# Attention and a routed MoE on one core: conditional weight loads, GpSimd drains, the left-over pass third, and the first slot's table and loads moved forward

## The chip, the core and the metric

The kernel runs on one core of one Trainium2 chip. The metric is device time in microseconds, the median of several runs. Engines are TensorE (PE, with its weight loads as PEld), VectorE (DVE), ScalarE (ACT), GpSimd (POOL) and SyncE (SP), which here only reads registers and issues DMAs. GpSimd issues the indirect DMAs (gathers and scatters by a list of row numbers).

## The reference

Sigmoid attention over 8 batches of 12 heads (448 positions, head size 64) gives x; each of its 3584 rows goes to the one expert of eight with the largest logit, through two matrices, and is scaled by two gates.

```python
# q, k, v: [8, 12, 448, 64]
scores = matmul(q, k.T) / sqrt(64) - log(448)
x = (sigmoid(scores) @ v).transpose(0, 2, 1, 3).reshape(3584, 768)
logits = x @ w_gate                       # [3584, 8]
e_idx = argmax(logits, axis=1)
gate_w = softmax(logits)[arange, e_idx]   # denominator + 1e-9
eom = sigmoid(x @ w_output_gate)
for e in range(8):
    mask = e_idx == e
    h = maximum(x[mask] @ w1[e], 0)       # 768 -> 1024
    out[mask] = gate_w[mask] * eom[mask, e] * (h @ w2[e])   # 1024 -> 768
```

## The kernel before

**Attention.** The work is 24 groups of two head pairs, each group seven units, 168 units in all, in one loop whose order is written out by hand. In turn `u` PE runs the scores of unit u (L540), ACT their sigmoid (L541), and PE the values of unit u-2 (L548). `evict` adds up and transposes a head pair's result (L561, L562); at a batch's end four DMAs write the batch to `x_dram` (L567). `gates(g-1)` runs in a group's fourth unit: PE multiplies the finished x by the gate weights `wg` (L580), and DVE adds that to `gl` (L584, L586). `load_qk` and `load_v` fetch two groups ahead.

**Routing.** `route(b)` is a generator whose steps the loop takes at fixed units: "logits" (L217 to L224), "counts" (L227 to L238), "places" (L240 to L252), "rows" (L254 to L260). The last one has GpSimd scatter the rows' numbers and gate values of batch b to the expert's region of a list in DRAM (`lst`, L258), four indirect DMAs. `init_list` fills that list beforehand.

**Slots.** The MoE part works in slots of 448 rows of one expert ("full") and of 256 rows ("part"). Two early full slots take rows of the first six batches only, so that slot 0 can be got ready while attention runs; the others are late ones. `table()` computes on DVE which expert and which place in the list each slot has. For a slot, `load_list` reads the place into an SP register and loads its list (L344), `spread_lists` copies it into `lts` and `lxs` on GpSimd (L351 to L354), `slot_regs` reads the expert into a register, `gather` fetches the rows (L363: 14 indirect DMAs for a full slot, 8 for a part slot), `turn_x` transposes them on DVE (L397). `load_w` loads weights into the raw area (L368), w1 and w2 in turn, since they share it. Every product is made as three: `split` makes a rounded part on ACT (L381) and the rest of it on DVE (L382).

**One slot.** `slot(cur, nxt)` starts with the gather of the next slot, then runs layer 1 in eight blocks f0 to f7 of 18 matmuls (L412 to L414, evicted by ACT L422 and DVE L423), meanwhile splitting the slot's own w2 and loading the next w1, then layer 2 in row tiles of 128 by two halves of 384 columns (L437 to L439, evicted by ACT L440), each tile scattered to `out` by GpSimd (L445), meanwhile turning and splitting the next x and w1 and loading the next w2. A full slot has 64 rows left over; `layer2_rest` (L458 to L461) takes them last.

**Slot 0.** Its steps stand inside the attention loop. In `unit(u)` u counts backward from the end of attention, -1 being the last unit with scores. The table's steps and the gather come from `before` and `after`, at the turn in which a pair index reaches `READY`: in the same count the table stands at -29 and -25, list 0 and the registers at -24, the gather at -22, list 1 at -18. w1 is loaded in six rows from -20 to -15 and split by rows at -15, -13, -11, -10, -3, -1; x is turned at -7, -6, -5 and split one unit later each. The loop ends with f0's matmuls of slot 0 (`layer1_mm`) and the last `gates`. The last batch's routing, the late table and the late lists come from the generator `side()`, one step between blocks of the first slots; its first step ("logits" of the last batch) is taken ahead of slot 0's `slot()` call, so between f0 and f1.

**Late and part slots.** How many there are is known at run time. At least two late slots always run; those beyond, and all part slots, are nested `tc.If` blocks (L716, L723), and behind each nest there is a join at which every engine brings its semaphores to the value that they would have with every block run. Each slot prefetches the one behind it, whether that exists or not. With these inputs two early, five late and two part slots run.

The functions that the diff touches:

Of the kernel before, what the change touches and what calls it, by code (L numbers as in the profile page):

```python
# [22 lines left out]
E = 8  # L23
# [21 lines left out]
READY = (EARLY_BATCH + 1) * NPAIR + 3  # L45
# [11 lines left out]
class Kernel:  # L57
# [67 lines left out]
    def constants(self):  # L125
# [11 lines left out]
        self.wg = cp.tile([128, NPAIR, D], F32, name="wg")  # L137
        nc.gpsimd.memset(self.wg, 0.0)
        nc.gpsimd.dma_start(self.wg[:, :, 0:16], self.wgo)
# [123 lines left out]
    def table(self, late):  # L263
# [8 lines left out]
        pos, tab = t([1, n, E]), t([1, 2, n])  # L272
# [24 lines left out]
        if late:  # L297
            ohb, tb, tmb = t([1, E, E]), t([1, 3, E]), t([1, E, E])
            bb = lambda a: a.unsqueeze(1).broadcast_to([1, E, E])
            slb = self.slots[:, 0, 0:E].unsqueeze(2).broadcast_to([1, E, E])  # L300
            tt(ohb, slb, bb(base[:, 1]), ALU.is_ge)
            tt(tmb, slb, bb(end[:, 1]), ALU.is_ge)
            tt(ohb, ohb, tmb, ALU.subtract)
            tt(tmb, ohb, bb(self.ids), ALU.mult)
            v.tensor_reduce(tb[:, 0], tmb, AX.X, ALU.add)
            tt(tmb, ohb, bb(sel[:, 1]), ALU.mult)
            v.tensor_reduce(tb[:, 1], tmb, AX.X, ALU.add)
            yield 1
# [9 lines left out]
        v.tensor_reduce(tab[:, 1], pos, AX.X, ALU.add)  # L318
        if late:
            first = t([1, n])  # L320
            v.tensor_scalar(first, self.slots[:, 0, 0:n], end[:, 0, E - 1:E], 0.0, ALU.is_equal, ALU.add)
            for i in range(2):
                v.scalar_tensor_tensor(tab[:, i], first, tb[:, i, 0:1], tab[:, i], ALU.mult, ALU.add)
            yield 1
        tabi = keep("tabi", [1, 2, n], I32)
        v.tensor_copy(tabi, tab)
        if late:
            tot, tbi = keep("tot", [1, 2], I32), keep("tbi", [1, 2, E], I32)
            v.tensor_copy(tot, end[:, :, E - 1])
            v.tensor_copy(tbi, tb[:, 0:2])  # L330
            self.tab_l, self.tab_b, self.tot = tabi, tbi, tot
        else:
            self.tab_e = tabi
# [33 lines left out]
    def load_w(self, s, src, dst, c, n):  # L367
        self.nc.sync.dma_start(  # L368
            dst[:, c:c + n],
            src[bass.ds(s["e"], 1), 128 * c:128 * c + 128 * n].rearrange("a (c p) f -> p (a c) f", p=128))  # L370
# [78 lines left out]
    def layer2_rest(self, s):  # L449
        nc = self.nc  # L450
        lt, (ya, yb) = s["lt"], self.ys
        lo, hi = slice(0, 64), slice(64, 128)
        for n in range(2):
            c = slice(384 * n, 384 * n + 384)
            ps = self.take("y", self.psy)[:, 0:384]
            for f in range(8):
                h = self.hr[:, f]
                nc.tensor.matmul(ps, h, self.w2h[:, f, c], start=(f == 0), stop=False)  # L458
                nc.tensor.matmul(ps, h, self.w2l[:, f, c], start=False, stop=(f == 7))
            nc.scalar.activation(yb[lo, c], ps[hi], AF.Copy, scale=r32(lt[hi, 3, 1:2]))  # L460
            nc.vector.scalar_tensor_tensor(ya[lo, c], ps[lo], r32(lt[lo, 3, 1:2]), yb[lo, c], ALU.mult, ALU.add)  # L461
        self.scatter(lt[lo, 3, 0:1], ya[lo])

    def slot(self, cur, nxt, side=None, begun=False):
        nx = None
        if begun:
            for k in range(4):
                self.load_w2(cur, k)
        if nxt is not None:
            nx = self.slot_regs(*nxt[:4])  # L470
            self.gather(nx, *nxt[4:])
        n = 32 * cur["lx"].shape[1]
# [14 lines left out]
        for i in range(2 * (n // 128)):  # L487
            t = i // 2
            self.layer2(cur, t, i % 2, self.ys[t % 2])
            if i == 0:  # L490
                self.split_x(nx, 2)
            if i < 3 and nx is not None:
                self.split_w1(i)
                for k in range(i, 4 if i == 2 else i + 1):
                    self.load_w2(nx, k)
            if side is not None and i > 0:
                next(side, None)
        if n % 128:
            self.layer2_rest(cur)
        return nx  # L500

    def attention(self, pool):
# [13 lines left out]
        self.es = self.scratch = t("es", [128, 1024])  # L516
        half = [slice(0, 64), slice(64, 128)]
# [59 lines left out]
        def gates(g):  # L577
            gp = self.ps_o[1]
            for h, e in corners:
                nc.tensor.matmul(gp[h][half[e], 0:S], self.wg[half[h], (G * g + e) % NPAIR], xts[e][half[h]],  # L580
                                 start=True, stop=True)
# [19 lines left out]
        for u in range(U * NG + LAG):  # L601
# [3 lines left out]
            if i == 0 or i == 4:  # L605
                self.before(G * g + i // 4)
# [14 lines left out]
            if i == 3 or i == 6:  # L621
                self.after(G * g + i // 4)
# [4 lines left out]
    def before(self, n):  # L627
        if n == READY + 2:
            self.early_slot()

    def unit(self, u):
        s = self.s0 if u > -21 else None
# [6 lines left out]
        for k in range(3):  # L639
            if u == -6 + k:  # L640
                self.split_x(s, k)
            if u == -7 + k:
                self.turn_x(s, k)
# [6 lines left out]

    def early_slot(self):
        self.early_lists(0, 1)
        self.s0 = self.slot_regs(self.tab_e, 0, self.lts[:, 0], self.lxs[:, 0])

    def after(self, n):
        if n == 2:
            self.init_list()
        if n == READY:
            self.tgen = self.table(False)
        if n == READY or n == READY + 1:  # L660
            for _ in range(2 - (n - READY)):
                next(self.tgen)
        if n == READY + 2:
            self.gather(self.s0, ROWS_E)
        if n == READY + 3:
            self.early_lists(1, EARLY)

    def build(self, phases="abc"):
# [14 lines left out]
        early = lambda k: (self.tab_e, k, self.lts[:, k], self.lxs[:, k], ROWS_E)  # L683
        late = lambda k: (self.tab_l, k, self.lts[:, EARLY + k], self.lxs[:, EARLY + k])

        def side():
            for _ in rt:
                yield
            yield
# [15 lines left out]
        next(sd)  # L705
# [15 lines left out]
        mid = lambda k: (self.tab_b, k, self.ltb[:, k], self.lxb[:, k])  # L721
# [41 lines left out]
```

## Time and profile before

| | us |
|---|---|
| median of 3 runs | 822.64 (822.46 to 823.29) |
| profiled run | 823.52 |
| its span | 821.7 |
| PE busy | 786.4 (96% of the span) |
| DVE, ACT, POOL busy | 380.7, 376.1, 287.1 |
| PE's first matmul of slot 0 (L412) starts | 298.56 |
| PE's first matmul of the first part slot starts | 732.00 |
| last scatter is issued | 802.58 |

Everything below is read from the one profiled execution. PE is the engine that is nearly always busy. The granted clock of PE over the span is 0.979 of full speed; it is lower where the page's row PEclk shows less than 9. A row of waits names the engine that waited, its line, and the engine and line whose work ended the wait.

### The profile page before, as it was taken

Reading aid. Unit: us, or ns where it says so; the run is one execution under the profiler, and the core shown is the slowest. Engines: PE = TensorE matmul, PEld = TensorE weight load, DVE = VectorE, ACT = ScalarE, POOL = GpSimd, SP = SyncE. Lnnn points to the kernel's source line nnn. Section 1 sums busy time; section 2 is a strip of 40 time slices with the busy share of each in tenths; the row PEclk is TensorE's granted clock in tenths of the full one; section 3 lists DMA queues with packets and bytes.
Section 4 is the critical chain, followed back from the end, with each engine's and each line's share of the span. In section 5 each row is a group of like instructions: output and inputs, shape, how many; then the busy total and the mean of one; then the engine's idle time right before and its main releaser. Section 6 shows DMA issues by size and latency. Waiting matters only on the chain. (4 is left out here: it accounts for less than half of the span.)

```text
span 821.7 us, 14599 instructions
## 1 busy us (share of the span) xinstructions
PE 786.4 (96%) x5748; PEld 598.7 (73%) x5748; DVE 380.7 (46%) x578; ACT 376.1 (46%) x437; POOL 287.1 (35%) x499
## 2 busy tenths in 40 slices
PE   9999999999999779999999999999999999989990
PEld 4444444444344349999999999999999999979990
DVE  1454444444454663925525615605615614616650
ACT  5656656666655632624424514514523523515540
POOL 5021213122135773128728027036136035124520
PEclk9999999999999988999999999999999999999995
DMA  8465664746667445562655346346345335425653
GB/s 289 123 169 137 186 147 141 202 114 162 159 175 214 145 101 189 164 206 60 196 199 180 123 150 202 107 139 207 100 141 202 119 126 197 141 95 183 236 204 131
DMA packets 75365, 132.78 MB, mean 162 GB/s; under 512 B 15487, under 2 KB 53375, under 8 KB 75280
## 3 DMA queue, kind: packets, MB, share of 16 engines
q1 hardware_dynamic: 64672, 106.47, 42.7%
q0 software_dynamic: 9680, 24.53, 9.3%
q8 instruction: 49, 0.80, 0.4%
q10 hardware_dynamic: 928, 0.69, 0.4%
q14 instruction: 36, 0.29, 0.1%
HBM read 108.77 MB, written 23.09 MB: 160 GB/s over the span
## 5 line engine op out<-in xcount | busy, mean ns | idle before, releaser
L541 ACT ACTIVATE a<-ps,bias_s 128x896 f32<-128x896 f32 x168 | 168.9, 1007 | 106.3 <-PE ps L540 106.3
L548 PE MATMUL ps<-a,v 64*64 64x448 f32 x1344 | 160.0, 542 | 3.9 <-ACT pc L240 3.9
L540 PE MATMUL ps<-q,k 64*64 64x448 f32 x1344 | 159.6, 544 | 2.4 <-ACT a L541 2.4
L412 PE MATMUL ps<-rounded 128*128 128x448 f32 (+1 forms) x432 | 152.8, 354 | 4.0 <-DVEq L716 4.0
L413 PE MATMUL ps<-rounded 128*128 128x448 f32 (+1 forms) x432 | 152.5, 353 | 0.0
L414 PE MATMUL ps<-rounded 128*128 128x448 f32 (+1 forms) x432 | 152.2, 352 | 0.0
L363 POOL DMA_INDIRECT plain<-x_dram,lxs x112 | 133.7, 1194 | 34.1 <-issue 33.7
L437 PE MATMUL ps<-w2h,h 128*128 128x384 f32 x400 | 133.7, 334 | 0.0
L438 PE MATMUL ps<-w2l,h 128*128 128x384 f32 x400 | 133.7, 334 | 0.0
L439 PE MATMUL ps<-w2h,h 128*128 128x384 f32 x400 | 133.7, 334 | 0.0
L382 DVE TENSOR_TENSOR rounded<-plain,rounded 128x2048 fp32r<-128x2048 f32 (+3 forms) x63 | 97.6, 1570 | 36.6 <-ACT rounded L381 36.6
L422 ACT ACTIVATE h<-ps 128x448 fp32r<-128x448 f32 (+1 forms) x72 | 36.7, 509 | 169.6 <-PE ps L414 155.2
L548 PEld LDWEIGHTS ps<-a,v 64*64 64x64 f32 x1344 | 53.3, 134 | 79.9 <-issue 73.4
L540 PEld LDWEIGHTS ps<-q,k 64*64 64x64 f32 x1344 | 50.7, 134 | 72.0 <-issue 65.5
L445 POOL DMA_INDIRECT out<-y,lts x28 | 29.7, 1060 | 208.2 <-ACT y L440 127.3
L381 ACT CAST rounded<-plain 128x2048 fp32r<-128x2048 f32 (+3 forms) x63 | 83.1, 1333 | 35.3 <-DVE plain L397 25.4
L423 DVE SCALAR_TENSOR_TENSOR h<-ps,h 128x384 fp32r<-128x384 f32 (+2 forms) x128 | 45.3, 390 | 113.3 <-ACT h L422 113.3
L412 PEld LDWEIGHTS ps<-rounded 128*128 128x128 f32 x432 | 82.9, 192 | 11.2 <-issue 5.0
L414 PEld LDWEIGHTS ps<-rounded 128*128 128x128 f32 x432 | 82.9, 192 | 6.3
L413 PEld LDWEIGHTS ps<-rounded 128*128 128x128 f32 x432 | 83.0, 192 | 6.2
L438 PEld LDWEIGHTS ps<-w2l,h 128*128 128x128 f32 x400 | 75.1, 188 | 0.1
L437 PEld LDWEIGHTS ps<-w2h,h 128*128 128x128 f32 x400 | 75.1, 188 | 0.1
(145 smaller groups left out, 724.8 us busy)
## 6 DMA issues: line engine op xcount, KB each, us to landing
plain<-w SPq DMA_DIRECT2D x40, 768.0 KB, 5.1
plain<-w SPq DMA_DIRECT2D x27, 1024.0 KB, 5.5
k<-kT SPq DMA_DIRECT2D x23, 448.0 KB, 4.6
q<-qT SPq DMA_DIRECT2D x23, 448.0 KB, 5.2
x_dram<-xt SPq DMA_DIRECT2D x30, 336.0 KB, 5.8
v<-vm SPq DMA_DIRECT2D x24, 384.0 KB, 4.7
plain<-w SPq DMA_DIRECT2D x6, 512.0 KB, 7.9
plain<-x_dram,lxs POOLq DMA_INDIRECT x112, 3.8
```

Of the source, the lines that this page charges most:

```text
L363: self.nc.gpsimd.indirect_dma_start(out=self.xg[:, g], out_offset=None, in_=x4, in_offset=bass.IndirectOffsetOnAxis(ap=s["lx"][:, g:g + 1] ...
L381: self.nc.scalar.copy(hi, raw)
L382: self.nc.vector.tensor_tensor(lo, raw, r32(hi), ALU.subtract)
L412: nc.tensor.matmul(ps, wh[d][:, c], xh[:, d, 0:n], start=(d == 0), stop=False)
L413: nc.tensor.matmul(ps, wh[d][:, c], xl[:, d, 0:n], start=False, stop=False)
L414: nc.tensor.matmul(ps, wl[d][:, c], xh[:, d, 0:n], start=False, stop=(d == 5))
L437: nc.tensor.matmul(ps, hh[:, f, tk], wh, start=(f == 0), stop=False)
L438: nc.tensor.matmul(ps, hh[:, f, tk], wl, start=False, stop=False)
L439: nc.tensor.matmul(ps, hl[:, f, tk], wh, start=False, stop=(f == 7))
L540: nc.tensor.matmul(ps[half[h], j, 0:S], k[half[j], e, o:o + 64], q[half[j], e], start=True, stop=True)
L541: nc.scalar.activation(at[u % 4], ps[:, :, 0:S], AF.Sigmoid, bias=self.bias_s, scale=1.0 / math.sqrt(D))
L548: nc.tensor.matmul(self.ps_o[e][h][half[j], 0:S], v[half[h], e, c, j], a[half[h], j], start=(i in ((0, 3 if h else 4)[e],)), stop=(i == (2 ...
```

## The change

- `load_w` takes a condition, and the DMA moves nothing where it is false. `table()` gets a third row that says whether a slot exists; `slot_regs` reads it into one more SP register for slots that may not exist (`sure=False`): late slots from the third on, and all part slots. The gather stays unconditional.
- Behind the gather of each such slot stands `gpsimd.drain()`.
- `layer2_rest` runs third in layer 2, behind the two halves of the first row tile; it uses one y buffer (y1), and the later tiles take the two in swapped order.
- In the attention loop the table of the early slots stands at u = -33, -32, -31, the registers at -30, w1's six loads from -30 to -25, list 0 at -28, the gather at -26, w1's row splits at -22, -20, ..., -12, list 1 at -17, turns at -11, -9, -7, the x splits at -9, -6, -4. Slot 0's w2 is loaded from -8 to -5 instead of at the start of `slot()`, and is split from f1 on, as in every other slot (before: from f3 on).
- `side()` starts with an empty step, so that the last batch's logits come behind f1 and its counts behind f2; everything later in it comes one step later.
- `wg` moves from the pool of constants to the pool of attention.

```diff
-        pos, tab = t([1, n, E]), t([1, 2, n])
+        pos, tab = t([1, n, E]), t([1, 3, n])
...
+            v.tensor_reduce(tb[:, 2], ohb, AX.X, ALU.add)
...
+        v.tensor_reduce(tab[:, 2], oh, AX.X, ALU.add)
...
-    def slot_regs(self, tab, k, lt, lx):
-        e = self.nc.values_load(tab[0:1, 0, k:k + 1], engines=[ET.SP], min_val=0, max_val=E - 1)
-        return dict(lt=lt, lx=lx, e=e)
+    def slot_regs(self, tab, k, lt, lx, sure=True):
+        ld = lambda r, hi: self.nc.values_load(tab[0:1, r, k:k + 1], engines=[ET.SP], min_val=0, max_val=hi)
+        return dict(lt=lt, lx=lx, e=ld(0, E - 1), cond={} if sure else dict(cond=ld(2, 1) > 0))
...
-            src[bass.ds(s["e"], 1), 128 * c:128 * c + 128 * n].rearrange("a (c p) f -> p (a c) f", p=128))
+            src[bass.ds(s["e"], 1), 128 * c:128 * c + 128 * n].rearrange("a (c p) f -> p (a c) f", p=128),
+            **s["cond"])
...
     def layer2_rest(self, s):
-        lt, (ya, yb) = s["lt"], self.ys
+        lt, y = s["lt"], self.ys[1]
...
-            nc.scalar.activation(yb[lo, c], ps[hi], AF.Copy, scale=r32(lt[hi, 3, 1:2]))
-            nc.vector.scalar_tensor_tensor(ya[lo, c], ps[lo], r32(lt[lo, 3, 1:2]), yb[lo, c], ALU.mult, ALU.add)
-        self.scatter(lt[lo, 3, 0:1], ya[lo])
+            nc.scalar.activation(y[lo, c], ps[hi], AF.Copy, scale=r32(lt[hi, 3, 1:2]))
+            nc.vector.scalar_tensor_tensor(y[lo, c], ps[lo], r32(lt[lo, 3, 1:2]), y[lo, c], ALU.mult, ALU.add)
+        self.scatter(lt[lo, 3, 0:1], y[lo])
...
     def slot(self, cur, nxt, side=None, begun=False):
-        if begun:
-            for k in range(4):
-                self.load_w2(cur, k)
         if nxt is not None:
-            nx = self.slot_regs(*nxt[:4])
-            self.gather(nx, *nxt[4:])
+            *at, rows, sure = nxt
+            nx = self.slot_regs(*at, sure)
+            self.gather(nx, rows)
+            if not sure:
+                self.nc.gpsimd.drain()
-        first = 3 if begun else 1
         for f in range(8):
             self.layer1(f, n, begun and f == 0)
-            k = f - first
-            if 0 <= k < 4:
-                self.split_w2(k)
-                if k:
-                    self.load_w1(nx, k - 1)
+            if 1 <= f < 5:
+                self.split_w2(f - 1)
+                if f > 1:
+                    self.load_w1(nx, f - 2)
...
-            self.layer2(cur, t, i % 2, self.ys[t % 2])
+            self.layer2(cur, t, i % 2, self.ys[(t + (t > 0 and n % 128 > 0)) % 2])
...
-        if n % 128:
-            self.layer2_rest(cur)
+            if i == 1 and n % 128:
+                self.layer2_rest(cur)
...
     def unit(self, u):
+        if u == -33:
+            self.tgen = self.table(False)
+        if -33 <= u < -30:
+            next(self.tgen)
+        if u == -30:
+            self.s0 = self.slot_regs(self.tab_e, 0, self.lts[:, 0], self.lxs[:, 0])
+        s = self.s0 if u >= -30 else None
         for d in range(6):
-            if u == -20 + d:
+            if u == -30 + d:
                 self.load_w(s, self.w1, self.w1r, d, 1)
-        for d, at in enumerate((-15, -13, -11, -10, -3, -1)):
-            if u == at:
+            if u == -22 + 2 * d:
                 self.split_w1_row(d)
+        if u == -28:
+            self.early_lists(0, 1)
+        if u == -26:
+            self.gather(s, ROWS_E)
+        if u == -17:
+            self.early_lists(1, EARLY)
+        for k, (a, b) in enumerate(((-11, -9), (-9, -6), (-7, -4))):
+            if u == a:
+                self.turn_x(s, k)
+            if u == b:
+                self.split_x(s, k)
+        if -8 <= u < -4:
+            self.load_w2(s, u + 8)
...
+        early = lambda k: (self.tab_e, k, self.lts[:, k], self.lxs[:, k], ROWS_E, True)
+        late = lambda k: (self.tab_l, k, self.lts[:, EARLY + k], self.lxs[:, EARLY + k], NT, k < LATE_MIN)
         def side():
+            yield
             for _ in rt:
                 yield
-            yield
...
         sd = side()
-        next(sd)
...
+        mid = lambda k: (self.tab_b, k, self.ltb[:, k], self.lxb[:, k], NT, False)
```

More of the change, by code (lines that the diff above doesn't have):

```diff
@@ L44 @@
 LG = 3
-READY = (EARLY_BATCH + 1) * NPAIR + 3
 OOB = 1 << 20
@@ L136, in constants @@
         make_identity(nc, self.ident)
-        self.wg = cp.tile([128, NPAIR, D], F32, name="wg")
-        nc.gpsimd.memset(self.wg, 0.0)
-        nc.gpsimd.dma_start(self.wg[:, :, 0:16], self.wgo)
         self.sel = cp.tile([128, 16], F32, name="sel")
@@ L321, in table @@
             v.tensor_scalar(first, self.slots[:, 0, 0:n], end[:, 0, E - 1:E], 0.0, ALU.is_equal, ALU.add)
-            for i in range(2):
+            for i in range(3):
                 v.scalar_tensor_tensor(tab[:, i], first, tb[:, i, 0:1], tab[:, i], ALU.mult, ALU.add)
             yield 1
-        tabi = keep("tabi", [1, 2, n], I32)
+        tabi = keep("tabi", [1, 3, n], I32)
         v.tensor_copy(tabi, tab)
         if late:
-            tot, tbi = keep("tot", [1, 2], I32), keep("tbi", [1, 2, E], I32)
+            tot, tbi = keep("tot", [1, 2], I32), keep("tbi", [1, 3, E], I32)
             v.tensor_copy(tot, end[:, :, E - 1])
-            v.tensor_copy(tbi, tb[:, 0:2])
+            v.tensor_copy(tbi, tb)
             self.tab_l, self.tab_b, self.tot = tabi, tbi, tot
@@ L516, in attention @@
         self.es = self.scratch = t("es", [128, 1024])
+        wg = t("wg", [128, NPAIR, D])
+        nc.gpsimd.memset(wg, 0.0)
+        nc.gpsimd.dma_start(wg[:, :, 0:16], self.wgo)
         half = [slice(0, 64), slice(64, 128)]
@@ L579, in gates @@
             for h, e in corners:
-                nc.tensor.matmul(gp[h][half[e], 0:S], self.wg[half[h], (G * g + e) % NPAIR], xts[e][half[h]],
+                nc.tensor.matmul(gp[h][half[e], 0:S], wg[half[h], (G * g + e) % NPAIR], xts[e][half[h]],
                                  start=True, stop=True)
@@ L604, in attention @@
                 load_qk(g + 2)
-            if i == 0 or i == 4:
-                self.before(G * g + i // 4)
             self.unit(u - U * NG)
@@ L620, in attention @@
                     routing(name)
-            if i == 3 or i == 6:
-                self.after(G * g + i // 4)
+            if u == 10:
+                self.init_list()
         self.layer1_mm(0, TB)
@@ L625, in attention @@
         return routes[-1]
-    def before(self, n):
-        if n == READY + 2:
-            self.early_slot()
     def unit(self, u):
-        s = self.s0 if u > -21 else None
+        if u == -33:
[5 more added lines that the diff above has]
+        s = self.s0 if u >= -30 else None
         for d in range(6):
-            if u == -20 + d:
+            if u == -30 + d:
                 self.load_w(s, self.w1, self.w1r, d, 1)
-        for d, at in enumerate((-15, -13, -11, -10, -3, -1)):
-            if u == at:
+            if u == -22 + 2 * d:
                 self.split_w1_row(d)
-        for k in range(3):
-            if u == -6 + k:
+        if u == -28:
[8 more added lines that the diff above has]
+            if u == b:
                 self.split_x(s, k)
-            if u == -7 + k:
-                self.turn_x(s, k)
+        if -8 <= u < -4:
+            self.load_w2(s, u + 8)
     def early_lists(self, a, b):
@@ L649, in early_lists @@
         self.spread_lists(lq[:, a:b], self.lts[:, a:b], self.lxs[:, a:b])
[L651 to L666, printed above, removed]
     def build(self, phases="abc"):
@@ L681, in build @@
             return
-        early = lambda k: (self.tab_e, k, self.lts[:, k], self.lxs[:, k], ROWS_E)
-        late = lambda k: (self.tab_l, k, self.lts[:, EARLY + k], self.lxs[:, EARLY + k])
+        early = lambda k: (self.tab_e, k, self.lts[:, k], self.lxs[:, k], ROWS_E, True)
+        late = lambda k: (self.tab_l, k, self.lts[:, EARLY + k], self.lxs[:, EARLY + k], NT, k < LATE_MIN)
         def side():
+            yield
             for _ in rt:
                 yield
-            yield
             self.scratch = self.hb
@@ L720, in build @@
                     cur = self.slot(cur, late(k + 1))
-        mid = lambda k: (self.tab_b, k, self.ltb[:, k], self.lxb[:, k])
+        mid = lambda k: (self.tab_b, k, self.ltb[:, k], self.lxb[:, k], NT, False)
         lists = lambda k: dict(lt=self.ltb[:, k], lx=self.lxb[:, k])
```

## The prediction

> **What bounds the kernel now.** I read the page first, then the waits, the chain that ended last, and the windows around each place that the diff touches.
>
> ```profile
> span 821.7 us, 14599 instructions
> ...
> PE 786.4 (96%) x5748; PEld 598.7 (73%) x5748; DVE 380.7 (46%) x578; ACT 376.1 (46%) x437; POOL 287.1 (35%) x499
> ...
> PE ps L412 <- DVEq L716: 4.0, 1, 4.0
> ...
> PE ps L540 <- ACT a L541: 2.4, 2, 2.1
> ...
> PE ps L232 <- DVE oh L224: 1.5, 1, 1.5
> ...
> PE ps L217 <- DVE gl L586: 1.5, 1, 1.5
> ```
>
> PE is busy for 96% of the span, so what can be won without taking work away is its few waits, its half-clock stretches, and what lies after its last matmul. A row of waits gives total, count and longest. These four and a wait of 3.94, below, are the largest of PE, and each lies at a place of the diff: the last units of attention, the start of slot 0, the join behind the late slots (L716). I take the places in order of time.
>
> **A. The last units of attention.** Columns: start, length, engine and line, and in brackets the idle time before and its releaser; a window's row has its bounds and length, the busy time of PE, PEld, DVE, ACT and POOL, the granted clock, the DMA share and GB/s.
>
> ```profile
> 265.86 0.93 PE L540 MATMUL ps<-q,k 64*64 64x448 f32 x8
> ...
> 271.47 1.26 PE L548 MATMUL ps<-a,v 64*64 64x448 f32 x6 [3.94 <-ACT pc L240]
> ...
> 298.56 0.47 PE L412 MATMUL ps<-rounded 128*128 128x448 f32 x1
> ...
> 302.46 0.98 PE L580 MATMUL ps<-x,wg 64*64 64x448 f32 x8
> ...
> L541 ACT ACTIVATE a<-ps,bias_s x5: 1007/1007/1007, 214.3 to 220.3; 128x896 f32<-128x896 f32 x5
> ...
> ACT rounded L381 <- DMA plain<-w: 5.5, 1, 5.5
> ...
> 272.00:276.00 4.00, 4.00 (x30) 1.72 (x28) 3.69 (x6) 3.83 (x5) 3.65 (x16) 0.57 0.86 318
> ...
> 290.00:297.00 7.00, 5.04 (x36) 2.91 (x40) 5.67 (x9) 6.02 (x7) 5.24 (x6) 0.76 0.20 57
> ```
>
> Unit u=-12 starts its scores at 265.86. Undisturbed, a unit takes 1.5 us (five sigmoids start 6.0 apart), so twelve units, two gate products of 0.98 and the last two units' values (1.5) would put slot 0's first matmul, L412, at about 287. It starts at 298.56: 11.5 us are lost to a row split (CAST, L381) that waits 5.5 us for w1, to the half clock after it, and to a backlog on ACT and DVE. The change loads w1 ten units earlier, so that wait goes. What is late next is the gathered x: turn_x, formerly from u=-7, now stands at u=-11, on DVE ahead of that unit's gate sums. The rows of the gather's own chain:
>
> ```profile
> 236.81 0.97 POOL L258 DMA_INDIRECT lst<-meta,posi  x1 [0.49 <-POOL meta L256]
> ...
> 247.10 0.93 POOL L258 DMA_INDIRECT lst<-meta,posi  x1 [1.39 <-DMA lst<-meta,posi]
> ...
> 249.21 0.37 SPq L344 DMA_DIRECT2D es<-lst  x1
> ...
> 254.80 1.00 POOL L363 DMA_INDIRECT plain<-x_dram,lxs  x1 [0.15 <-POOL lts L354]
> ...
> 271.24 0.94 POOL L363 DMA_INDIRECT plain<-x_dram,lxs  x1 [0.30 <-issue]
> ...
> DMA to landing us min/median/max: 2.6/6.3/9.2
> ...
> DMA to landing us min/median/max: 3.5/5.4/7.3
> ...
> 688.27 1.76 DVE L382 TENSOR_TENSOR w2l<-plain,w2h 128x1536 fp32r<-128x1536 f32 x1 [0.67 <-ACT w2h L381]
> ...
> 688.68 2.17 POOL L363 DMA_INDIRECT plain<-x_dram,lxs  x1 [0.31 <-issue]
> ...
> 282.00 1.07 DVE L397 STREAM_TRANSPOSE plain<-plain 128x896 f32<-128x896 f32 x1
> ...
> 245.81 1.35 DVE L586 TENSOR_TENSOR gl<-gl,ps 128x448 f32<-128x448 f32 x2 [1.78 <-PE ps L580]
> ```
>
> (The first landing row is L363's between 250 and 310, the second L344's.) The list is complete only when batch 5's four scatters have landed, one after the other, and nothing moves those; so the gather can't start earlier though its place in the code does. I expect it later: table steps on DVE now stand ahead of the reciprocal that lets the scatters go, and w1 on SP and the DMA engines ahead of the list's load, together an estimated 2.0 us (254.80 to 256.8). The fourteen issues span 16.44. Three row splits fall among them, and a gather beside a split takes 2.17 where the one at 271.24 takes 0.94: 1.2 each when they meet fully, half of that taken, 1.8. So the last issue is at 275.0, and with the 2.6 of an uncrowded landing x is there at R = 277.6. Then come the turn (1.07), the gate sums (1.35), and for PE eight units (12.0), a gate product, two units' values and a rest of 0.5 (3.0), and 2.5 of half clock, between one window (4.0 at 0.57: 1.7) and both (another 7.0 at 0.76: 1.7). L412 starts at R+19.9 = 297.5, so A gains only **1.0**. Ends: with scatters 2.3 apart, not 3.4 (3.3 earlier), no delay of 2.0 and no hold-up, R is 270.5, DVE is hardly blocked, and L412 starts near 288: +10. With the slow landings (7.3 for 3.5, 9.2 for 2.6) R is 288: -9.
>
> The Trainium skill, "SBUF — State Buffer", section "SBUF: two separate sides", calls the port pair that GpSimd and VectorE share an exclusive lock, held for the whole instruction, also against a VectorE operation with two SBUF inputs. It speaks against this change: by it three splits cost up to 3.6, not 1.8, and the result below would be 1.8 later; the row of 2.17 agrees with it, but no row shows how three would fall.
>
> **B. Start of slot 0.**
>
> ```profile
> 307.57 0.72 PE L412 MATMUL ps<-rounded 128*128 128x448 f32 x1
> ...
> 311.60 0.54 ACT L422 ACTIVATE h<-ps 128x448 fp32r<-128x448 f32 x1 [14.10 <-DMA x_dram<-xt]
> ...
> 307.60:313.80 6.20, 6.20 (x24) 5.54 (x21) 0.69 (x2) 0.90 (x4) 0.87 (x1) 0.57 0.99 315
> ```
>
> From f0's end (302.46) to f1 (307.57) PE runs the gates and the logits and waits 1.5 twice; f1 then runs at 0.57 of the clock and takes 6.2. With logits behind f1 and counts behind f2, both waits have a block of matmuls as cover, and f1 follows the gates without a gap: 1.45 + 1.50, and for the clock 2.5, between 2.3 (6.2 against f0's 3.9) and 2.7 (43% of 6.2). Gain **5.5**. Cover needed: ACT evicts f0 only when x_dram has landed, 13.0 after L412's start; f3 takes that bank again about 13.3 after it. Slot 0's w2 no longer loads beside it. End if that fails: 1 less.
>
> **C. Join behind the late slots.**
>
> ```profile
> L716 ACTq EVENT_SEMAPHORE  x1: 17/17/17, 730.7 to 730.7; - x1
> ...
> L716 DVEq EVENT_SEMAPHORE  x1: 21/21/21, 731.8 to 731.8; - x1
> ...
> L716 PEldq EVENT_SEMAPHORE  x1: 51/51/51, 728.6 to 728.6; - x1
> ```
>
> Each engine settles its semaphores at the join; PE's wait of 4.0 ends with DVE's step at 731.8, and DVE's last work before it is the left-over's add (L461). With the left-over third, DVE is there long before. Next is ACT at 730.7 (gain 1.1) or, if PE needs only DVE, PE itself at 728.6 (up to 3.1). I take the middle, **2.0**. A half-clock stretch follows the join now, and I leave it: one also follows L540's wait of 2.1 (the window from 290). The Trainium skill, "TensorE: Matmul & The Clock Gate", section "Part 1: The HAM clock gate", wants an idle window of some 3.4 us before the clock drops; by it the shorter gap would stay at full clock, and the result would be an estimated 1.7 less. The stretch behind the wait of 2.1 speaks against it.
>
> **D and E. After the last matmul.**
>
> ```profile
> 796.09 7.08 SPq L368 DMA_DIRECT2D plain<-w  x4
> ...
> 802.58 0.99 POOL L445 DMA_INDIRECT out<-y,ltb  x1 [5.65 <-ACT y L440]
> ...
> DMA to landing us min/median/max: 8.4/8.4/8.4
> ...
> DMA to landing us min/median/max: 3.0/3.0/3.0
> ...
> L723 POOLq INC_SWDGE_SEM  x1: 1913/1913/1913, 811.3 to 811.3; - x1
> ...
> L759 POOLq DRAIN  x3: 46/109/7177, 813.4 to 821.1; - x3
> ...
> L755 POOLq DRAIN  x1: 184/184/184, 0.4 to 0.4; - x1
> ```
>
> The first landing row is the last scatter's, the second that of a scatter near 365, with little traffic. The chain that ended last is nothing but the last two scatters. D: the last one lands after 8.4, beside w2 loads (L368) of a slot that doesn't exist. With these loads conditional I take 4.0, near the quiet one since nothing else is left to move: gain **4.4**. Ends: 5.4 by the quiet row, 2.1 by the 6.3 of gathers in traffic.
>
> E: GpSimd's last DRAIN takes 7.18; the one at the start, before any DMA of its own, 0.18. If it walks what GpSimd issued since the last drain (112 gathers of late and early slots alone), the new drains behind six gathers leave it two scatters: gain **7.0**. If it is a fixed cost of the end: 0. I take 7.0, because the GpSimd DMAs behind them are the one difference that I find between the two. The 1.9 just ahead of it I leave. Inside the slots a drain sits between the gather and the first scatter, where POOL idles:
>
> ```profile
> 706.74 1.39 POOL L445 DMA_INDIRECT out<-y,lts  x1 [14.64 <-ACT y L440]
> ...
> 794.49 2.45 POOL L445 DMA_INDIRECT out<-y,ltb  x1 [11.59 <-ACT y L440]
> ```
>
> So even a drain of 7.2 behind a gather landing in 2.6 is hidden. If it weren't, scatters, then y, then PSUM would hold PE.
>
> Edits at nothing: the third row of the tables (one or two DVE reductions), two register loads for a slot on SP, which idles between loads, wg's new pool, and side's steps one place later (lists are ready a slot ahead). Were SP full, the register loads would delay w1.
>
> **Sum.** 1.0 + 5.5 + 2.0 + 4.4 + 7.0 = 19.9. The profiled run took 823.52 (span 821.7), so 803.6 on its own basis; the median shown is 0.88 below that: **802.7**.
>
> **Rivals.**
> 1. The final drain stays (fixed, or drains settle nothing): 802.7 + 7.0 = 809.7. For it: only one long drain in the trace.
> 2. x isn't late: A gives 10, not 1: 793.7. For it: crowding of the list's chain is my estimate.
> 3. x is later still, by w1's traffic: A gives -8: 811.7.
> 4. The conditional loads don't deliver (the queue moves data regardless, D at 0: 807.1), or x_dram lands late again and half-clocks f1 (B at 0: 808.2).
> 5. Slower: the new drains hold GpSimd past its slack. Six drains have 11.6 to 14.6 us of idle each, 13.1 in the mean; to undo 19.9 and be seen (1.6 more), each must take over 13.1 + 3.6 = 16.7 us. With 20 each: 802.7 + 6 x 6.9 = 844. Against it: the longest drain in the trace is 7.2.
>
> **How the numbers follow.** Forecast 0.50, rival 1 0.18, 2 0.12, 3 0.10, 4 0.07, 5 0.03. The likeliest one alone spans 799.5 to 805.5. The range 794.5 to 811 leaves out 3, 5 and half of 2, about 0.19. A measurement here tells 0.2% (1.6 us). Faster has every case but the last and a mishap beside it: 0.94; same 0.02; slower 0.04.
>
> **What will show it.** A: the gather's first and last issue near 256.8 and 275, a DVE turn waiting for DMA till 277 to 278, L412 near 297.5; wrong if PE shows no wait there. B: no wait at L217 and L232, f1 near 3.7. C: a wait at L716 of about 2, not on DVE. D: one L368 group fewer after 790, a landing near 4. E: L759's longest DRAIN under 0.5 and drains in the slots with no new PE wait. The sum fails first at E, then at A.

## The result and the profile after

| | before | after |
|---|---|---|
| median, us | 822.96 (822.46 to 823.93) | 809.62 (808.85 to 810.65) |
| profiled run, its span | 823.52, 821.7 | 810.65, 809.0 |
| granted clock over the span | 0.979 | 0.987 |

The ratio is 0.9837, with a 95% interval of 0.982 to 0.9854: faster by 13.3 us. The forecast was 19.9 faster (802.7, range 794.5 to 811.0). More than the whole gain comes from the end of the program, a little from the join; attention and the start of slot 0 got longer. The experiments ran on other chips, where the kernel before took 837 to 840 us, so they are compared by ratios to it, by kernels that ran on the same chip, and by stages of the traces; what the traces show of these slower chips stands at the end, and its cause stays open.

Where the two profiled spans differ, by the start of PE's matmuls (f0 to f7 are slot 0's blocks of layer 1):

| stretch | before | after | gain | forecast |
|---|---|---|---|---|
| start to f0 (A) | 298.56 | 301.79 | -3.2 | 1.0 |
| f0 to layer 2 of slot 0 (B) | 37.1 | 37.5 | -0.4 | 5.5 |
| from there to the end of the last late slot | 392.3 | 392.3 | 0 | 0 |
| join and two blocks behind it (C) | 9.9 | 7.3 | 2.6 | 2.0 |
| the rest of the part slots | 63.7 | 63.7 | 0 | 0 |
| PE's end to the end (D, E) | 20.1 | 6.4 | 13.7 | 11.4 |

The waits of PE in the changed kernel (total, times, longest), which answer to the first rows shown of before. L411 is the line that was L412, L705 the join that was L716, L228 the counts that were L232.

```profile
PE ps L548 <- DVE gl L586: 11.0, 1, 11.0
PE ps L228 <- DVE oh L220: 4.2, 1, 4.2
PE ps L411 <- ACTq L705: 2.9, 1, 2.9
```

The waits for logits and counts of 1.5 each and that at the join's DVE are gone; two larger ones stand in other places. For the first one, the chain from list to f0 in the changed kernel's timeline (start, length, engine, line, idle before) and the landing of the fourteen gathers:

```profile
248.03 0.94 POOL L254 DMA_INDIRECT lst<-meta,posi  x1 [6.08 <-DMA lst<-meta,posi]
...
253.39 0.36 SPq L342 DMA_DIRECT2D es<-lst  x1
...
258.38 1.00 POOL L361 DMA_INDIRECT plain<-x_dram,lxs  x1 [0.15 <-POOL lts L352]
...
270.24 2.38 SPq L366 DMA_DIRECT2D plain<-w  x4
...
275.38 0.94 POOL L361 DMA_INDIRECT plain<-x_dram,lxs  x1 [0.30 <-issue]
...
281.42 1.11 DVE L396 STREAM_TRANSPOSE plain<-plain 128x896 f32<-128x896 f32 x1 [12.17 <-DMA plain<-x_dram,lxs]
...
283.82 1.02 PE L548 MATMUL ps<-a,v 64*64 64x448 f32 x3 [10.96 <-DVE gl L586]
...
301.79 0.47 PE L411 MATMUL ps<-rounded 128*128 128x448 f32 x1
```

```profile
DMA to landing us min/median/max: 5.0/6.1/7.0
```

The gather starts 3.6 later than before (254.80), x lands at 281.4, DVE stands at the first turn for 12.2, and PE behind it for 11.0. SyncE issued slot 0's w2 at 270.24, ahead of the last five gathers. In the kernel before, where w1's loads stood beside them, the same fourteen gathers landed like this:

```profile
DMA to landing us min/median/max: 4.8/6.4/7.0
```

The second one, counts behind f2, in the timelines of ACT, DVE and PE, and two windows (bounds, length, busy PE, PEld, DVE, ACT, POOL, granted clock, DMA share, GB/s):

```profile
313.65 0.54 ACT L421 ACTIVATE h<-ps 128x448 fp32r<-128x448 f32 x1 [12.91 <-DMA plain<-x_dram,lxs]
...
314.22 1.28 DVE L422 SCALAR_TENSOR_TENSOR h<-ps,h 128x384 fp32r<-128x384 f32 x4 [6.21 <-ACT h L421]
316.02 1.76 DVE L381 TENSOR_TENSOR w2l<-plain,w2h 128x1536 fp32r<-128x1536 f32 x1 [0.51 <-ACT w2h L380]
317.69 0.22 DVE L214 COPY lg<-ps 112x64 f32<-112x64 f32 x1
...
318.91 0.19 DVE L220 TENSOR_TENSOR oh<-rk,fi 112x32 bf16<-112x32 f32 x1
...
319.15 0.18 PE L228 MATMUL ps<-oh,tri 112*128 112x32 bf16 x1 [4.23 <-DVE oh L220]
```

```profile
306.50:311.00 4.50, 4.50 (x30) 4.18 (x27) 1.24 (x2) 0.00 (x0) 3.28 (x5) 1.00 0.86 197
311.00:319.20 8.20, 3.97 (x22) 3.43 (x22) 4.23 (x12) 4.61 (x8) 0.76 (x1) 1.00 0.31 94
319.30:324.70 5.40, 5.40 (x27) 4.86 (x25) 2.06 (x3) 0.00 (x0) 0.00 (x0) 0.68 0.42 120
```

f1 and the logits' matmuls now run at full clock in 4.5 (f1 alone took 6.2). But the logits' result is read by DVE only at 317.69: ahead of it in DVE's queue stand the evictions of f0 and f1, which wait for ACT and ACT for DMAs until 313.65, and the first split of w2. PE idles 4.23, and the next block runs at 0.68 of the clock.

The end of the program: the last scatter, its landing, and the groups of three lines (count, ns min/median/max, first and last start):

```profile
803.52 0.99 POOL L444 DMA_INDIRECT out<-y,ltb  x1 [6.97 <-ACT y L439]
```

```profile
DMA to landing us min/median/max: 3.4/3.4/3.4
```

```profile
L712 POOLq INC_SWDGE_SEM  x1: 213/213/213, 807.1 to 807.1; - x1
...
L748 POOLq DRAIN  x3: 46/109/309, 807.8 to 808.7; - x3
...
L470 POOLq DRAIN  x6: 10001/16936/18207, 502.5 to 778.8; - x6
```

8.4 became 3.4, 1.91 became 0.21, and 7.18 became 0.31. The records of the six new drains (L470) last 10 to 18 us, since each begins while gathers ahead of it are still being issued. Only 2.4 to 5.3 us of each lie behind the last of these gathers, the next scatter comes at least 5.7 later, and no wait of PE goes back to them.

### The profile page after: what moved, and what is told of

It reads as the page before. It is cut to its first block, busy times and chain, and to the rows that moved or that the text cites. A ratio compares the mean times of both kernels' runs of the same rounds, so it can differ in the third digit from the quotient of the medians.

```text
span 809.0 us, 14609 instructions
## 1 busy us (share of the span) xinstructions
PE 782.8 (97%) x5748; PEld 596.7 (74%) x5748; DVE 380.7 (47%) x582; ACT 374.9 (46%) x437; POOL 290.8 (36%) x499
## 5 line engine op out<-in xcount | busy, mean ns | idle before, releaser
L548 PE MATMUL ps<-a,v 64*64 64x448 f32 x1344 | 164.5, 541 | 11.0 <-DVE gl L586 11.0
L540 PE MATMUL ps<-q,k 64*64 64x448 f32 x1344 | 164.9, 543 | 0.4 <-ACT a L541 0.4
L411 PE MATMUL ps<-rounded 128*128 128x448 f32 (+1 forms) x432 | 151.8, 351 | 2.9 <-ACTq L705 2.9
L412 PE MATMUL ps<-rounded 128*128 128x448 f32 (+1 forms) x432 | 151.3, 350 | 0.0
L361 POOL DMA_INDIRECT plain<-x_dram,lxs x112 | 136.2, 1217 | 33.8 <-issue 33.4
L381 DVE TENSOR_TENSOR rounded<-plain,rounded 128x2048 fp32r<-128x2048 f32 (+3 forms) x63 | 97.7, 1573 | 61.1 <-ACT rounded L380 61.0
L540 PEld LDWEIGHTS ps<-q,k 64*64 64x64 f32 x1344 | 52.4, 134 | 70.0 <-issue 66.5
L411 PEld LDWEIGHTS ps<-rounded 128*128 128x128 f32 x432 | 81.9, 190 | 10.7 <-ACTq L705 3.2
L413 PEld LDWEIGHTS ps<-rounded 128*128 128x128 f32 x432 | 81.9, 190 | 6.3
L412 PEld LDWEIGHTS ps<-rounded 128*128 128x128 f32 x432 | 81.9, 190 | 6.1
```

Source lines behind the costliest of these rows:

```text
L361: self.nc.gpsimd.indirect_dma_start(out=self.xg[:, g], out_offset=None, in_=x4, in_offset=bass.IndirectOffsetOnAxis(ap=s["lx"][:, g:g + 1] ...
L381: self.nc.vector.tensor_tensor(lo, raw, r32(hi), ALU.subtract)
L411: nc.tensor.matmul(ps, wh[d][:, c], xh[:, d, 0:n], start=(d == 0), stop=False)
L412: nc.tensor.matmul(ps, wh[d][:, c], xl[:, d, 0:n], start=False, stop=False)
L413: nc.tensor.matmul(ps, wl[d][:, c], xh[:, d, 0:n], start=False, stop=(d == 5))
L540: nc.tensor.matmul(ps[half[h], j, 0:S], k[half[j], e, o:o + 64], q[half[j], e], start=True, stop=True)
```

## The experiments

**The end: drains and conditional loads.** Three kernels on one chip; before was at 838.71 there.

```diff
 no_drains (changed kernel)
-            if not sure:
-                self.nc.gpsimd.drain()
 drains_late_only (changed kernel)
-            if not sure:
+            if not sure and nx["lx"].shape[1] == GB_:
 before_plus_cond (kernel before)
+            **s["cond"])      # with the tables' third row, its register, and wg moved
```

> The changed kernel without its six drains. Theory 1: GpSimd's last DRAIN takes as long as it has GpSimd DMAs behind it since the last drain; then it is back at about 7.2 us (0.31 with the drains) and the semaphore step ahead of it at about 1.9 (0.21), nothing changes for PE, and the time is 809.6 + 8.6 = 818. Rival: the last DRAIN got short because the loads of the slot that doesn't exist are gone; then it stays at 0.3 and the time at 809.6. Second rival: the drains, which hold GpSimd 2.4 to 5.3 us behind each gather, cost something that I don't see; then the time is below 818 by that much.

> The changed kernel with drains only behind the gathers of 448 rows, none in the two part slots. Behind the last drain that is left come 24 GpSimd DMAs (4 scatters, 8 gathers, 2 scatters, 8 gathers, 2 scatters), of 194 in all. Theory 1, in proportion to their number: 7.0 x 24/194 = 0.9 more than the shortest, so a last DRAIN of about 1.1 us and a time of 809.6 + 0.9 = 810.5. Rival: a drain anywhere resets something, and the last one stays at 0.3. Rival: only one right behind the last gather helps, and the last one is near 7.2 (818).

> The kernel before with the conditional loads alone (and the weight tile of the gates moved to the attention pool, to make room for the longer tables). Theory: the last scatter lands after about 3.4 us, not 8.4, the last DRAIN stays at 7.2 and nothing else changes: 5.0 faster than before, about 818. Rival: the landing got short because the drains had emptied GpSimd's queue; then it stays at 8.4 and the time at 823.

Measured: 826.26, ratio 0.9839 (0.98 to 0.9877); 817.43, 0.9751 (0.9721 to 0.978); 835.18, 0.9957 (0.9936 to 0.9977). The semaphore step and the last drain of each, in this order of kernels, and the last scatter of the third:

```profile
L710 POOLq INC_SWDGE_SEM  x1: 1913/1913/1913, 815.6 to 815.6; - x1
...
L746 POOLq DRAIN  x3: 109/194/7177, 817.7 to 825.7; - x3
```

```profile
L712 POOLq INC_SWDGE_SEM  x1: 647/647/647, 809.4 to 809.4; - x1
...
L748 POOLq DRAIN  x3: 46/109/2090, 810.5 to 813.1; - x3
```

```profile
L727 POOLq INC_SWDGE_SEM  x1: 1913/1913/1913, 824.4 to 824.4; - x1
...
L763 POOLq DRAIN  x3: 46/109/7177, 826.5 to 834.2; - x3
```

```profile
820.36 0.99 POOL L445 DMA_INDIRECT out<-y,ltb  x1 [7.25 <-ACT y L440]
```

Without drains the last DRAIN is back at 7177 ns, with or without the loads of the missing slot, so the drains alone shorten it, by 6.87, and the semaphore step by 1.70. With 24 GpSimd DMAs behind the last drain it takes 2.09, against 0.31 with two. It grows with their number, as theory 1 has it, but not in proportion (1.1 was expected): if the number alone decides, it levels off before 194. Where, and whether something else decides, no run shows. In total no_drains is 8.8 above drains_late_only, 7.1 of it behind PE's end (15.7 against 8.6); the changed kernel itself wasn't run on this chip. The conditional loads alone bring the semaphore step 4.0 behind the last scatter, against 8.7 before: the landing is theirs, not the drains'. Stage and total agree here only roughly: 0.9957 is 3.6 us, where the landing gave 4.7.

**The logits' place.** On the same chip:

```diff
 logits_before_f1 (changed kernel)
         def side():
-            yield
...
         sd = side()
+        next(sd)
```

> The changed kernel with the last batch's logits ahead of f1 again, as before. Theory: the new wait of 4.2 us on the counts, and the half clock behind it (f2 and f3 1.9 longer together), come from DVE's order: the logits' steps stand behind f0's eviction, which waits for the DMAs out of the attention pool. With the old order that wait is gone and the two old ones of 1.5 each are back, with half clock in f1: f0 to layer 2 takes 37.1, not 37.5, and the time stays at 809.3. Rival: the counts wait for something else (the gate sums, or PE's order); then the wait of 4.2 stays in this kernel too, and the old ones come on top: 812 to 815.

Measured: 822.58, ratio 0.9812 (0.9775 to 0.985). PE's waits:

```profile
PE ps L213 <- DVE gl L586: 9.1, 1, 9.1
...
PE ps L228 <- DVE oh L220: 2.4, 2, 1.5
```

The counts' wait of 4.2 is gone and one of 1.5 is back, as the theory has it; but the logits wait 9.1 where 1.5 was expected, since the gate sums on DVE had waited 8.0 for what the profile calls only "remote" (the last section tells what these waits are). f0 to layer 2 takes 47.4. The run doesn't price the edit.

**Where x's landing and the turn stand.** after_again (the changed kernel unedited), turns_back, w2_later and, further down, evict_behind_logits ran on one chip, before at 837.08; w2_back, turns_m5 and turns_m5_evict on another, before at 840.03.

```diff
 turns_back
-        for k, (a, b) in enumerate(((-11, -9), (-9, -6), (-7, -4))):
+        for k, (a, b) in enumerate(((-7, -6), (-6, -5), (-5, -4))):
 w2_later
-        if -8 <= u < -4:
-            self.load_w2(s, u + 8)
+        if -4 <= u < 0:
+            self.load_w2(s, u + 4)
 w2_back: slot 0's w2 loads at the start of slot(), split from f3 on, as before
 turns_m5
+        for k, (a, b) in enumerate(((-5, -4), (-4, -3), (-3, -1))):
```

> The changed kernel unedited, as the measure for the three beside it. From its first profile: first turn done near 282, f0 at 301.8 (35.9 behind the scores of u=-12), f0 to layer 2 37.5, join 2.9, 6.4 from PE's end to the end of the span; some 1.6% below before.

> The changed kernel with x turned at u=-7, -6, -5 and split one unit later each, as before. Theory: the stall of 11 us on PE is the first turn, which holds DVE at u=-11 until x has landed (281.4); four units further on, PE has 6 us less of work behind it when x lands, so f0 starts 4 to 6.5 us earlier (near 296) and the time falls by as much. Rival: what the turn no longer blocks comes back as a backlog of three turns and three splits on DVE and ACT ahead of f0, as in the kernel before; then f0 is at most 2 earlier.

> The changed kernel with slot 0's four w2 loads at u=-4 to -1, not -8 to -5. Theory: these 3 MB, issued from 270.2 to 272.4, share the DMA engines with the last gathers of x (last issue 275.4, landed 281.4, where 2.6 would be 278.0); without them x lands near 278 and f0 starts about 3.4 earlier, so does the end. Rival: the crowd is x_dram and v of the last batches, issued from 258 to 268; then x lands at 281 all the same and the time stays.

> The changed kernel with slot 0's w2 loaded at the start of slot 0 and split from f3 on, as before. The kernel with these loads at u=-4 to -1 showed that SyncE runs ahead of the units: three of the four loads went out from 269.5 to 272.4 all the same, and x landed at 281.4 again. Here they stand behind the DMAs of x_dram, which wait for the last batch. Theory: with these 3 MB gone from 270 to 283 the last gather lands in 2.6 to 3.5, not 6.0: the first turn starts at 278 to 279, not 281.5, and from the scores of u=-12 to f0 it takes 3 less than in the changed kernel on the same chip; f0 to layer 2 grows by up to 3, since w2 then loads beside x_dram. Rival: the crowd is x_dram and v of the batches before; then the turn stays at 281.5.

> The changed kernel with x turned at u=-5, -4, -3 and split at -4, -3, -1. Theory: u=-5 starts about 277.2, so DVE reaches the first turn within 2 to 3 us of x's landing at 281.4 and PE's stall of 11 us shrinks to 0 to 2; f0 starts near 291 to 293, not 301.8, and the time falls by 8 to 10 us. On a chip where PE loses time to its own issue in these units, as on the two before, PE reaches u=-5 some 6 later and the gain is that much smaller. Rival: the three turns and splits, now in five units, hold up DVE and ACT, and f0's first blocks wait for them: gain below 3.

Measured: after_again 818.7, ratio 0.9781 (0.9728 to 0.9834); turns_back 816.25, 0.9752 (0.9699 to 0.9805); w2_later 817.5, 0.9743 (0.9688 to 0.9799); w2_back 818.98, 0.9754 (0.9697 to 0.9811); turns_m5 817.6, 0.9713 (0.9671 to 0.9756). The intervals overlap, so the totals decide nothing; the first turn does. SyncE's loads in w2_later, then the first turn of w2_later and of w2_back:

```profile
269.68 12.28 SPq L366 DMA_DIRECT2D plain<-w  x4
...
281.48 1.10 DVE L396 STREAM_TRANSPOSE plain<-plain 128x896 f32<-128x896 f32 x1
```

```profile
278.81 1.11 DVE L396 STREAM_TRANSPOSE plain<-plain 128x896 f32<-128x896 f32 x1 [1.40 <-DMA plain<-x_dram,lxs]
```

Moving the loads four units back in the code moved three of the four nowhere in time: SyncE, whose queue had nothing to wait for, began issuing them at 269.68. Only the fourth, which overwrites w1's last row, went out at 281.6, behind that row's split. (The turn at 281.48 has no wait in its row: DVE came to it then, and x was there.) Only behind the x_dram DMAs (w2_back) do all four leave the crowd, and x lands 2.7 behind the last gather's issue (276.09), not 6.0. The DMA packets of the fourteen gathers agree. The last one ends 2.3 behind the last issue in w2_back and in w2_held (below), the two kernels that keep w2 out of the crowd, and 3.5 to 5.8 behind it in the ten that don't, 5.0 and 4.7 in turns_m5 and turns_m5_evict on w2_back's own chip. So w2 is what made x late, by about 3.

What that is worth at f0 isn't shown. From the scores of u=-12 to f0 w2_back takes 28.5, after_again 32.5 on another chip, and the changed kernel 35.9 in its first profile; but two kernels whose edits don't touch this stretch have 24.5 (no_drains) and 34.1 (drains_late_only). From f0 to layer 2 w2_back takes 44.5, after_again 42.1.

The turn's place stays undecided. In turns_back and turns_m5 no turn holds PE, but f0 doesn't come earlier either (302.9 and 304.4). The stall of 11 us isn't there in after_again either: on these chips PE, DVE and ACT lost time in the same units, and DVE got to the first turn at 281.57, when x was just there.

**The eviction's place on DVE.** On the chips of after_again and of turns_m5:

```diff
 evict_behind_logits (changed kernel), turns_m5_evict (turns_m5): slot 0's f0 and f1
         for f in range(8):
-            self.layer1(f, n, begun and f == 0)
+            if begun and f == 0:
+                first = self.h_ps
+                next(side)
+                continue
+            if begun and f == 1:
+                self.layer1_mm(1, n)
+                next(side)
+                second, self.h_ps = self.h_ps, first
+                self.layer1(0, n, True)
+                self.h_ps = second
+            self.layer1(f, n, begun and f == 1)
```

> The changed kernel with f0's eviction emitted behind the logits' step (ACT and DVE both), all else as it is. Theory: the counts wait 4.2 us because the logits' six steps stand behind f0's eviction on DVE, and that one waits for DMAs out of the attention pool until about 313.6; ahead of it they are done by 312.5, so the wait of 4.2 and the half clock behind it (1.9) are gone, f3 takes f0's bank just as it comes free, and f0 to layer 2 takes 31.5 to 33, not 37.5: 4.5 to 6 us less. Rival: f3 waits for f0's bank in its place, until about 315 plus what the landing is late, and 1 to 2 us are left. Second rival: PE's wait was not DVE's order; then nothing changes.

> The kernel with the turns at u=-5, -4, -3 and, as well, f0's eviction emitted behind the logits' step. Theory: both gains, some 8 to 10 at f0 and 4 to 6 between f0 and layer 2, as far as f3 doesn't wait for f0's bank: 12 to 15 us below the changed kernel where PE's issue is undisturbed (near 796). Rival: with f0 earlier relative to the landing of x_dram and of slot 1's gather, f3 waits, and the second gain is under 2.

Measured: 815.04, ratio 0.9719 (0.967 to 0.9767), beside after_again's 0.9781; 818.32, 0.9721 (0.9673 to 0.9769), beside turns_m5's 0.9713. In after_again the last batch's counts didn't wait for DVE, since PE itself was late in f2, so evict_behind_logits had no such wait to remove: f0 to layer 2 takes 41.7 there and 42.1 in after_again, where 31.5 to 33 was expected. The counts' matmul in turns_m5, and in turns_m5_evict with the step that it waits for:

```profile
326.83 0.18 PE L228 MATMUL ps<-oh,tri 112*128 112x32 bf16 x1 [3.67 <-DVE oh L220]
```

```profile
319.96 0.23 DVE L214 COPY lg<-ps 112x64 f32<-112x64 f32 x1 [10.06 <-remote]
...
321.43 0.18 PE L228 MATMUL ps<-oh,tri 112*128 112x32 bf16 x1 [0.36 <-DVE oh L220]
```

The edit takes DVE's evictions from ahead of the logits, and the wait of 3.67 is down to 0.36. But DVE took up the logits only at 319.96, for another reason that is named only "remote", and PE's own matmuls came late meanwhile. f0 to layer 2 is 40.9 against 43.1, the totals are level: the mechanism is supported by this one pair, and its price where nothing else stalls was not measured.

**A version with the three together.** Alone on its chip, before at 838.98:

```diff
 w2_held (changed kernel, with the eviction's edit)
-            if u == -22 + 2 * d:
+            if u == (-8 if d == 1 else -22 + 2 * d):
                 self.split_w1_row(d)
-        for k, (a, b) in enumerate(((-11, -9), (-9, -6), (-7, -4))):
+        for k, (a, b) in enumerate(((-6, -5), (-5, -4), (-4, -2))):
```

> The changed kernel with three edits: the split of w1's second row at u=-8, so that w2's loads, which overwrite that row, can't be issued before (SyncE ran ahead to 270 otherwise); turns of x at u=-6, -5, -4 and splits at -5, -4, -2; f0's eviction emitted behind the logits' step. Theory: w2's 3 MB move out of the crowd at 270 to 283 into the quiet stretch from 284 on, x lands at 278 to 279, no turn holds PE by more than 2 us, and the counts don't wait for f0's eviction. Where the engines aren't short of instructions, f0 starts near 289 to 292 and f0 to layer 2 takes 32 to 34: about 795. Where they are, as in the last three sessions (all engines idle near 265 to 278 and 310 to 320 with the DMA engines full), those stretches stay, and the time is 3 to 6 us below the changed kernel: a ratio to before of 0.967 to 0.972. Rival: on such a chip the crowd of the batches before alone sets both stretches; then the ratio is that of the changed kernel, 0.978.

Measured: 814.24, ratio 0.9707 (0.968 to 0.9735). SyncE's w2 loads, and the counts:

```profile
286.17 2.55 SPq L366 DMA_DIRECT2D plain<-w  x4
...
321.27 0.18 PE L228 MATMUL ps<-oh,tri 112*128 112x32 bf16 x1 [8.16 <-DVE oh L220]
```

The held row split does move w2 to 286, the gathers' last packet ends at 278.90, and f0 starts at 299.97. The counts' wait of 8.16 is not one for the evictions, which stand behind the logits here: DVE took up the logits at 319.80, after 13.5 named "remote". f0 to layer 2 takes 42.9, where 32 to 34 was expected on a chip without such stretches. The ratio is inside what was expected and the lowest of all, with turns_m5's 0.9713 close to it. Against the changed kernel's 0.9781 on another chip the intervals overlap: that it beats the kernel before is shown, that it beats the change is likely and not shown.

## Why the prediction was right or wrong

The sign and the range held: 809.62 lies in 794.5 to 811.0. That it falls on the figure of rival 1 (809.7) is chance: rival 1 had the last drain stay, and it went. A and B fell short of the forecast by 4.2 and 5.9; the end and C exceeded it by 2.3 and 0.6. Of that, 1.7 is a semaphore step and 1.5 a stretch at full clock, both of which the sum had at nothing, so that the range held in part by luck.

**A failed in the landing.** The list came late, as forecast, and the last issue at 275.38 is the 275.0 of the working; from x's landing to f0 it took 20.4, where 19.9 was worked out. The wrong term is the landing, 2.6 taken and 6.0 measured. It was taken from the quiet end of a row whose median, 6.3, was shown beside it, on the ground that the gather would be uncrowded. That row runs to 310, and its quiet end belongs to slot 1's gathers: slot 0's own took 4.8 and more already before. And the working has no term for slot 0's w2. In the code it stands at u=-8, behind the first turn; SyncE runs ahead of the units, and issued it at 270.24. w2_back undoes that and has the turn at 278.8.

That the last issue fits so well is partly chance: the list came 1.6 later than forecast, and the fourteen issues gave 1.2 of it back, with 17.0 from first to last, 0.6 more than before and not 1.8. One of the list's scatters waited 6.1 for the one before it (3.7 before), beside w1's loads. And two steps of the list's own chain met a row split (L381), which the working had beside the gathers alone:

```profile
250.18 1.23 DVE L381 TENSOR_TENSOR rounded<-plain,rounded 128x1024 fp32r<-128x1024 f32 x1
...
250.36 1.85 POOL L254 DMA_INDIRECT lst<-meta,posi  x1 [1.39 <-DMA lst<-meta,posi]
...
256.21 1.22 DVE L381 TENSOR_TENSOR rounded<-plain,rounded 128x1024 fp32r<-128x1024 f32 x1
...
256.36 1.12 POOL L349 COPY lxs<-es 32x14 int32<-32x14 int32 x1
...
268.07 1.18 DVE L381 TENSOR_TENSOR rounded<-plain,rounded 128x1024 fp32r<-128x1024 f32 x1
...
268.71 1.36 POOL L361 DMA_INDIRECT plain<-x_dram,lxs  x1 [0.30 <-issue]
```

The scatter takes 1.85 (0.93 before) and the copy 1.12 (0.19 before). Of the gathers three met a split, and took 1.06, 1.11 and 1.36. Each of them ends 0.82 behind the split's end, as did the gather of 2.17 that the prediction shows: a meeting costs what is left of the split when the gather begins. The exclusive lock in the Trainium skill, "SBUF — State Buffer", section "SBUF: two separate sides", fits these rows; the estimate of up to 3.6 that was worked out from it for three full meetings does not, since here they were partial and cost 0.6.

**B failed in its cover.** Both old waits went and f1 ran at full clock, as forecast. "Both waits have a block of matmuls as cover" counted PE's blocks and the bank of f0, but not DVE's queue, where the logits' steps now stand behind the evictions of f0 and f1 and behind the first split of w2, which the same change had moved to f1. That cost 4.2 of wait and about 1.7 of half clock in the block behind it (5.3 against 3.65). The rivals had "x_dram lands late again", but as f3's wait for a bank. Here a late landing (the row at 313.65 names slot 1's gather, not x_dram, as the last) holds f0's eviction, and through DVE's queue the logits; before, the logits stood ahead of that eviction on DVE. This is read from the changed kernel's own rows, in which each step follows the one before it with at most 0.5 between; how much of the wait is the evictions' and how much the split's, no run separates.

**C came near its figure by two errors.** PE now waits for ACT, so that the wait gave the lower of the two ends, 1.1, not the middle of 2.0. Another 1.5 came from the clock, which the sum had left as it was. In this profile the blocks behind the gap of 2.9 ran at full clock:

```profile
735.20:738.80 3.60, 3.60 (x33) 3.60 (x32) 0.42 (x1) 0.38 (x1) 0.00 (x0) 1.00 0.03 9
```

That is what the rule on the idle window in the Trainium skill, "TensorE: Matmul & The Clock Gate", section "Part 1: The HAM clock gate", would have, and what I had set aside. But the same kernel, on another chip and with a gap of 2.7, shows:

```profile
739.80:743.40 3.60, 3.60 (x21) 3.60 (x20) 0.43 (x1) 0.38 (x1) 0.00 (x0) 0.57 0.02 6
```

Over the twelve kernels with the left-over third, gaps of 2.6 to 2.9 at this join were followed by full clock three times and by a half-clock stretch nine times, in no order of length. That section of the Trainium skill also says that the window runs freely, and gives it a length of some 3.4. A gap of 2.6 to 2.9 is shorter than that wherever it falls, so the nine cases go against the rule, and the measurements decide. They give a chance, three in twelve, not a term; what decides between the two, no run shows.

**D and E were right.** 5.0 for the landing (4.4 forecast), 6.9 for the drain (7.0), and 1.7 for the semaphore step that the sum had left out. The drains' cover in the slots held: PE's stretch from layer 2 of slot 0 to the join is 392.3 in both.

## What to carry to other kernels

A step's place in the program is its place in time only on a queue that something holds; a DMA queue that waits for nothing runs ahead, and a load must be tied to data (here a row that it overwrites) to come late. When a step is moved behind cover on one engine, list what stands ahead of its parts on each other engine's queue too, what else the same change has put there, and what the first of these waits for. And read the end of the program as a stage of its own: here a drain, a semaphore step and a landing gave all of the gain.

## What the runs showed of the hardware

- GpSimd's last DRAIN took 7.18 us with no drain behind a gather, 2.09 with 24 of its DMAs since the last one, 0.31 with two. The semaphore step ahead of it went with it: 1.91, 0.65, 0.21.
- On the chips of the experiments PE, DVE and ACT lost time together in stretches around 265 to 280 and 310 to 320, where the profile names no releaser ("issue" on PE, "remote" on the others). GpSimd went on: it issued its gathers 1.25 apart, as elsewhere, where the expectation of w2_held has all engines idle. Two such stretches, of after_again and of w2_held:

```profile
270.00:274.00 4.00, 1.95 (x7) 0.74 (x5) 0.00 (x0) 0.00 (x0) 2.92 (x4) 0.83 0.92 263
...
314.00:318.00 4.00, 0.00 (x0) 0.00 (x0) 0.00 (x0) 0.00 (x0) 2.54 (x3) 0.78 0.31 81
```

Every "remote" row in these traces is a wait for PE's semaphore. In after_again ACT and DVE go on at 278.16 and 278.35, behind updates of it at 278.14 and 278.32, while the records of the PE steps that they wait for end at 267.05 and 269.07. In the first two profiles each update follows its record within 0.1. So in these stretches either PE's signals were late or its records are early, and its records can't be read as the time of its work. A busy DMA alone isn't the cause: in the first profile of the changed kernel, which like that of the kernel before has no "remote" row, PE was busy throughout with a DMA share of 1.08:

```profile
264.00:272.00 8.00, 8.00 (x93) 3.41 (x90) 4.36 (x6) 5.85 (x10) 6.17 (x7) 1.00 1.08 355
```

The Trainium skill, "Runtime: NRT & Kernel Launch", section "Instruction fetch mechanics", says that the engines fetch their instructions by DMA, in blocks of 16 KiB; the instruction queue q8 on the profile's page (49 packets, 0.80 MB) agrees with that size. Late blocks of instructions could be a cause, but the trace speaks against them: in after_again the two instruction queues moved no packet from 266 to 284 and none from 304 to 333, so none came at the end of a stretch. What the cause is, and why the first chip was spared, stays open, and with it the price of B's and the turn's edits.
